# Reordering the first half of an attention kernel around its loads, splitting the third products, and moving three x copies to ScalarE

## The chip, the cores and the metric

The kernel runs on one core of one Trainium2 chip. The metric is the device time of one execution in microseconds (us). Every run also gives a span, from the first to the last instruction that the profile shows; it is 1.7 to 3.4 us shorter than the device time. Times inside a trace count from the start of the span. A run counts as slow when it lies more than 1.5% above the fastest of the same kernel in its call; comparisons use fast runs unless the text says otherwise.

## The reference, cut to what matters

A linear attention with a decay per head (4 batches, 8 heads, 768 positions, head width 64), whose output, as x of 4 x 768 x 512, goes through a token mixer. The kernel computes the attention in chunks of 128 positions.

```python
for b in range(nb):                      # blocks of positions
    intra = ((qb @ kb^T) * Dmask) @ vb
    inter = (qb * lam_pow) @ kv_state
    out[block] = intra + inter
    kv_state = lam_block * kv_state + (kb * rev_pow)^T @ vb
# ... x = out, heads side by side
wq, wk = x @ w_q, x @ w_k                # 512 -> 64
W_tok  = 1/sqrt(64) * wq @ wk^T          # 768 x 768, per batch
out    = relu(W_tok @ x) @ w_out
```

The kernel computes (wq wk^T) x as wq (wk^T x): **py** is wk^T x, its copy is **Y**, and the "third products" **pm** are Y times wq.

## The kernel before

One loop step n handles one pair of heads; there are 16 steps, four for each batch. `kk` is the place of the pair in its batch. The pieces, with the names by which the profile's rows show them:

- `load_more` issues on GpSimd the loads of q, k and v of a pair (fq, fk, fv) and scales v of an earlier pair (vn).
- `turn(n)` transposes q and k on TensorE (trq, trk); VectorE copies q (qT), ScalarE copies k (kT).
- `states(n)` (dps), `scores(n)` (sc, then four masks by VectorE into pr), `inter(n)` (first part of oa), `values(n)` (rest of oa, copied to xnat by ScalarE), `flip(n)` (xp, transposed x, copied to xT).
- The mixer: `mix_wk` (the k projection, wk), `mix_wq`, `mix_py`, `mix_pm` and the output products `mix_po` (po).

```python
def load_more(n):
    load_q(n)
    load_kv(n, "k")
    scale_v(n - 2, nc.gpsimd) if n - 2 > 3 else None
    load_kv(n, "v")

def flip(n):
    b, kk = pairs[n]
    xp = pst([128, NCH, CH], BF16, "xp")
    for t in range(NCH):
        nc.tensor.transpose(xp[:, t, :], xnat[b][:, t, kk * CH : (kk + 1) * CH], ident)
    # ... last pair: half on each engine
    elif n < 2:
        nc.scalar.copy(out=to, in_=xp)
    else:
        nc.vector.tensor_copy(out=to, in_=xp)

def mix_pm(b, which, ...):          # two values of "which" are four products, in four banks
    pms = [pst([128, HALF], F32, "pm") for _ in which]
    # ... one matmul each from Y and wqT, then a ScalarE relu of each into rmT

for n in range(N):
    b, kk = pairs[n]
    if 8 <= n + 6 < N:
        load_more(n + 6)
    # ...
    p = b - 1
    third = [2 * kk - 4, 2 * kk - 3] if b >= 1 and kk >= 2 else []
    outs = ...                      # which output products go into this step
    if n >= 1 and not third:
        inter(n - 1)
    scores(n)
    if n >= 1 and third:
        inter(n - 1)
    if third:
        mix_pm(p, third)
    masks(n, 0)
    masks(n, 1)
    if n >= 1:
        values(n - 1)
    if n >= 2:
        flip(n - 2)
    for i, t in outs:
        mix_po(i, t)
    if b >= 1 and kk == 1:
        mix_wk(p)
    if n <= 9:
        states(n)
        turn(n + 1)
    if 9 <= n < N - 1:
        states(n + 1)
    if 9 <= n < N - 2:
        turn(n + 2)
    # ...
    if b >= 1 and kk == 1:
        mix_wq(p)
        mix_py(p)
```

The order of the calls is the order of the instructions on every engine. Up to step 9 the turn of pair n+1 is the last thing of step n; step 9 is the "double step", which does the states and turns of two pairs, so that from step 10 on the turn runs two pairs ahead of the scores. All PSUM tiles come from one pool of 8 banks.

## Time and profile before

| | before |
|---|---|
| device time, median of 3 | 108.0 us (107.91 to 109.81) |
| the profiled run: device time, span | 106.78, 105.1 us |
| busy share of TensorE, VectorE, ScalarE, GpSimd | 81%, 64%, 60%, 64% |
| scores of pair 8 start | 46.56 us |
| states of pair 10 start | 56.96 us |
| inter of pair 15 (start of the unchanged tail) | 86.56 us |

A line of an engine's timeline reads: start, length, engine, source line, operation, output <- inputs, shape, and how many instructions are grouped. The bracket gives the idle time just before and what ended it. In the list of waits a row has the total, the number of times and the longest. The lines of this kernel are read in the prediction below. One group is added: the third products of step 10 in TensorE's timeline of the kernel before.

```profile
59.30 0.51 PE L284 MATMUL sc<-qT,kT 64*128 64x128 bf16 x12
...
60.60 0.50 PE L437 MATMUL pm<-wqT,Y 64*128 64x384 bf16 x3 [0.44 <-ACT Y L420]
```

Scores and inter stand between py and the third products, and cover most of the time that ScalarE needs for Y. 0.44 us is left uncovered.

### The profile page before, as it was taken

Reading aid. Unit: us, or ns where it says so; the run is one execution under the profiler, and the core shown is the slowest. Engines: PE = TensorE matmul, PEld = TensorE weight load, DVE = VectorE, ACT = ScalarE, POOL = GpSimd, SP = SyncE. Lnnn points to the kernel's source line nnn. Section 1 sums busy time; section 2 is a strip of 40 time slices with the busy share of each in tenths; the row PEclk is TensorE's granted clock in tenths of the full one; section 3 lists DMA queues with packets and bytes.
Section 4 is the critical chain, followed back from the end, with each engine's and each line's share of the span. In section 5 each row is a group of like instructions: output and inputs, shape, how many; then the busy total and the mean of one; then the engine's idle time right before and its main releaser. Section 6 shows DMA issues by size and latency. Waiting matters only on the chain.

```text
span 105.1 us, 3513 instructions
## 1 busy us (share of the span) xinstructions
PE 85.0 (81%) x1496; PEld 57.1 (54%) x1504; DVE 67.1 (64%) x168; ACT 63.4 (60%) x124; POOL 67.5 (64%) x69
## 2 busy tenths in 40 slices
PE   4957898776559868979749998999498999999960
PEld 1325786655448555465549675567385548443430
DVE  3247997895886677257486689397768485237240
ACT  4282458657331996756632999766349796658430
POOL 5999999699999999999999999735000000000000
PEclk9996559999999999999999999999999999999998
DMA  0999999999999999999999999998930142342584
GB/s 21 261 174 160 163 166 166 173 164 168 197 170 164 168 155 158 149 136 163 128 137 138 136 154 133 136 263 296 372 148 0 54 152 100 127 172 104 225 312 158
DMA packets 67440, 17.12 MB, mean 163 GB/s; under 512 B 62946, under 2 KB 64482, under 8 KB 67426
## 3 DMA queue, kind: packets, MB, share of 16 engines
q0 software_dynamic: 60400, 9.57, 123.3%
q1 hardware_dynamic: 6882, 7.21, 20.3%
q8 instruction: 11, 0.18, 0.8%
q10 hardware_dynamic: 144, 0.13, 0.4%
q14 instruction: 3, 0.02, 0.1%
HBM read 20.19 MB, written 6.29 MB: 252 GB/s over the span
## 4 chain that ended last, share of the span: by engine, by line
PE 43%; POOL 16%; ACT 14%; DVE 13%; DMA 8%; issue 3%; ACTq 0%; POOLq 0%; DVEq 0%
PE po L475 18%; DVE pr L297 8%; DMA fv<-in_v_dram 8%; ACT kT L241 5%; POOL fv L78 4%; POOL fk L78 4%; PE dps L254 4%; PE oa L325 3%; POOL fq L73 3%; ACT rmT L457 3%; PE wk L366 3%; PE xp L344 3%; POOL vn L192 3%; PE trk L237 3%; PE trq L218 3%
## 5 line engine op out<-in xcount | busy, mean ns | idle before, releaser
L297 DVE TENSOR_TENSOR pr<-sc,maskc 128x384 bf16<-128x384 f32 x64 | 31.2, 550 | 8.3 <-PE sc L284 8.3
L241 ACT COPY kT<-trk 128x768 bf16<-128x768 bf16 x16 | 12.8, 799 | 19.1 <-PE trk L237 18.8
L192 POOL TENSOR_TENSOR vn<-fv,DvI 128x768 bf16<-128x768 bf16 x14 | 21.0, 1500 | 3.8 <-DMA fv<-in_v_dram 3.4
L475 PE MATMUL po<-wo,rmT 128*128 128x512 bf16 (+1 forms) x92 | 22.3, 370 | 0.5
L78 POOL DMA_DIRECT2D fv<-in_v_dram x16 | 17.3, 1081 | 0.8 <-POOLq L612 0.8
L485 ACT COPY osb<-po 128x512 f32<-128x512 f32 (+1 forms) x22 | 12.6, 579 | 8.3 <-PE po L475 8.2
L337 ACT CAST xnat<-oa 128x384 bf16<-128x384 f32 x31 | 13.5, 493 | 4.8 <-PE oa L325 4.6
L78 POOL DMA_DIRECT2D fk<-in_k_dram x15 | 15.6, 1041 | 0.0
L475 PEld LDWEIGHTS <-rmT 128*128 128x128 bf16 x100 | 9.0, 98 | 9.5 <-issue 0.8
L457 ACT ACTIVATE rmT<-pm 128x384 bf16<-128x384 f32 x28 | 11.7, 493 | 1.7 <-PE pm L437 1.6
L73 POOL DMA_DIRECT2D fq<-in_q_dram x15 | 12.7, 847 | 0.0
L284 PE MATMUL sc<-qT,kT 64*128 64x128 bf16 x192 | 8.7, 228 | 4.8 <-ACT kT L241 3.8
L284 PEld LDWEIGHTS <-kT 64*128 64x128 bf16 x192 | 6.1, 99 | 6.5 <-ACT kT L241 4.7
L218 PE MATMUL trq<-ident,fq 128*64 128x128 bf16 x192 | 9.0, 231 | 0.6 <-DVE fq L501 0.6
L224 DVE TENSOR_TENSOR qT<-trq,dq 128x768 bf16<-128x768 bf16 x16 | 8.8, 549 | 0.9 <-PE trq L218 0.9
L325 PE MATMUL oa<-vn,pr 128*128 128x64 bf16 x192 | 8.7, 197 | 0.0
L325 PEld LDWEIGHTS <-pr 128*128 128x128 bf16 x192 | 6.7, 100 | 3.5 <-issue 2.6
L237 PE MATMUL trk<-ident,fk 128*64 128x128 bf16 x180 | 8.0, 226 | 0.7 <-DMA fk<-in_k_dram 0.7
L437 PE MATMUL pm<-wqT,Y 64*128 64x384 bf16 x32 | 6.8, 327 | 2.1 <-ACT Y L420 1.3
L264 DVE COPY two<-dps 128x64 f32<-128x64 f32 x16 | 3.5, 218 | 7.7 <-PE dps L254 7.7
L352 DVE COPY xT<-xp 128x768 bf16<-128x768 bf16 x13 | 7.2, 552 | 1.5 <-PE xp L344 1.5
L344 PE MATMUL xp<-ident,xnat 128*128 128x128 bf16 x96 | 8.0, 219 | 0.0
(61 smaller groups left out, 110.7 us busy)
## 6 DMA issues: line engine op xcount, KB each, us to landing
out_dram<-osb SPq DMA_DIRECT2D x23, 256.0 KB, 2.1
fv<-in_v_dram POOLq DMA_DIRECT2D x16, 192.0 KB, 6.2
fq<-in_q_dram POOLq DMA_DIRECT2D x15, 192.0 KB, 5.7
fk<-in_k_dram POOLq DMA_DIRECT2D x15, 192.0 KB, 6.1
wo<-in_moe_w_out_dram POOLq DMA_DIRECT2D x1, 512.0 KB, 7.9
k<-in_k_dram SPq DMA_DIRECT2D x1, 384.0 KB, 3.6
q<-in_q_dram SPq DMA_DIRECT2D x1, 384.0 KB, 5.4
wqk_f<-in_moe_w_q_dram SPq DMA_DIRECT2D x1, 128.0 KB, 6.4
```

The costliest lines, as they stand in the source:

```text
L73: nc.gpsimd.dma_start(out=t, in_=q_rows(n))
L78: nc.gpsimd.dma_start(out=t, in_=kv_rows(n, dict(k=k, v=v)[nm]))
L192: eng.tensor_tensor(out=vn, in0=staged.pop((n, "v")), in1=DvI[:, 2 * kk : 2 * kk + 2, :].unsqueeze(3).to_broadcast([128, 2, NCH, D]), op=A ...
L218: nc.tensor.transpose(trq[hl * 64 : hl * 64 + 64, 2 * a : 2 * a + 2, r, :], fq[:, hl, a, r * D : (r + 1) * D], ident,)
L241: nc.scalar.copy(out=kT, in_=trk)
L284: nc.tensor.matmul(sc[a, hl][:, cc, :], kT[r, c * CH : (c + 1) * CH], qchunk(n, r, c), start=True, stop=True, skip_group_check=True,)
L297: nc.vector.tensor_tensor(out=t, in0=L[n]["sc"][a, hl], in1=maskc, op=ALU.mult)
L325: nc.tensor.matmul(oa[hl][:, c, :], pr[c // 3, hl][:, c % 3, :], vn[:, hl, c, :], start=False, stop=(c == NCH - 1), skip_group_check=True,)
L337: nc.scalar.copy(out=to, in_=oa[hl])
L457: nc.scalar.activation(out=to, in_=pm, func=ACT.Relu, scale=1.0 / 8.0)
L475: nc.tensor.matmul(po, M[b]["rmT"][:, kt, t * CH : (t + 1) * CH], wo[:, kt, c : c + w], start=(kt == 0), stop=(kt == 3),)
L485: nc.scalar.copy(out=osb[:, c : c + w], in_=po)
```

## The change

The intent is to put work that needs nothing new between a transposition and the reader of its copy, so that TensorE does not wait for copies, and to feed the mixer's projections earlier. There are five parts. No instruction is added or taken away; three x copies change from VectorE to ScalarE (steps 4, 9 and 13).

1. In steps 1 to 3 and 5 to 7, states and turn come ahead of values, flip and po ("the whole-array phase behind the turn").
2. The first k projection moves from step 5 to step 4, its wq and py into the middle of step 5. For this, x of pair 3 is turned in step 4 already, and x of pair 2 is copied by ScalarE.
3. The double step moves from 9 to 8, one po from 8 to 9.
4. In steps 9 and 13 x is turned before values and copied by ScalarE. In step 13, too, a po now stands ahead of wk: it is taken from step 14.
5. In steps where kk is 2 or 3, half of the third products stand ahead of scores and half behind inter.

```diff
-    def flip(n):
+    def flip(n, eng=None):
...
-        elif n < 2:
+        elif eng is nc.scalar:
             nc.scalar.copy(out=to, in_=xp)
...
-        third = [2 * kk - 4, 2 * kk - 3] if b >= 1 and kk >= 2 else []
-        outs = {7: [...], 8: [(0, 3), (0, 4), (0, 5)], N - 1: [(2, 0)]}.get(n)
+        outs = {7: [...], 8: [(0, 3), (0, 4)], 9: [(0, 5)], 10: [], N - 1: [(2, 0)]}.get(n)
...
-            outs = [..., [], [(p - 1, 4), (p - 1, 5)], ...][kk]
+            outs = [..., [(p - 1, 4)], [(p - 1, 5)], ...][kk]
...
+        def back():
+            if kk == 1 and n > 8:
+                flip(n - 2, nc.scalar)
+            if n >= 1:
+                values(n - 1)
+            if n >= 2 and not (kk == 1 and n > 8) and n != 5:
+                flip(n - 2, nc.scalar if n < 5 else None)
+            if n == 4:
+                flip(n - 1)
+            for i, t in outs:
+                mix_po(i, t)
+            if kk == 1 and n > 8:
+                mix_wk(p)
-        if n >= 1 and not third:
+        if n >= 1 and not (b >= 1 and kk >= 2):
             inter(n - 1)
-        scores(n)
-        if n >= 1 and third:
+            scores(n)
+        elif n >= 1:
+            mix_pm(p, [2 * kk - 4])
+            scores(n)
             inter(n - 1)
-        if third:
-            mix_pm(p, third)
+            mix_pm(p, [2 * kk - 3])
+        else:
+            scores(n)
         masks(n, 0)
         masks(n, 1)
-        # values, flip, outs, mix_wk stood here
-        if n <= 9:
+        if n == 4 or n >= 8:
+            back()
+        if n <= 8:
             states(n)
+        if n == 5:
+            mix_wq(p)
+            mix_py(p)
+        if n <= 8:
             turn(n + 1)
-        if 9 <= n < N - 1:
+        if 8 <= n < N - 1:
             states(n + 1)
-        if 9 <= n < N - 2:
+        if 8 <= n < N - 2:
             turn(n + 2)
...
-        if b >= 1 and kk == 1:
+        if kk == 1 and n > 8:
             mix_wq(p)
             mix_py(p)
+        if n == 4:
+            mix_wk(p)
+        elif n < 8:
+            back()
```

More of the change, by code (lines that the diff above doesn't have):

```diff
@@ L531 @@
         p = b - 1
-        third = [2 * kk - 4, 2 * kk - 3] if b >= 1 and kk >= 2 else []
-        outs = {7: [(0, 0), (0, 1), (0, 2)], 8: [(0, 3), (0, 4), (0, 5)], N - 1: [(2, 0)]}.get(n)
-        if outs is None:
-            outs = [
-                [(p - 1, 2), (p - 1, 3)],
-                [],
-                [(p - 1, 4), (p - 1, 5)],
-                [(p, 0), (p, 1)],
-            ][kk]
-            outs = [(i, t) for i, t in outs if i > 0]
-        if n >= 1 and not third:
+        outs = {
+            7: [(0, 0), (0, 1), (0, 2)],
+            8: [(0, 3), (0, 4)],
+            9: [(0, 5)],
+            10: [],
+            N - 1: [(2, 0)],
+        }.get(n)
+        if outs is None:
+            outs = [[(p - 1, 2), (p - 1, 3)], [(p - 1, 4)], [(p - 1, 5)], [(p, 0), (p, 1)]][kk]
+            outs = [(i, t) for i, t in outs if i >= 0]
+        def back():
[12 more added lines that the diff above has]
+        if n >= 1 and not (b >= 1 and kk >= 2):
             inter(n - 1)
-        scores(n)
-        if n >= 1 and third:
+            scores(n)
+        elif n >= 1:
+            mix_pm(p, [2 * kk - 4])
+            scores(n)
             inter(n - 1)
-        if third:
-            mix_pm(p, third)
+            mix_pm(p, [2 * kk - 3])
+        else:
+            scores(n)
         masks(n, 0)
         masks(n, 1)
-        if n >= 1:
-            values(n - 1)
-        if n >= 2:
-            flip(n - 2)
-        for i, t in outs:
-            mix_po(i, t)
-        if b >= 1 and kk == 1:
-            mix_wk(p)
-        if n <= 9:
+        if n == 4 or n >= 8:
+            back()
+        if n <= 8:
             states(n)
+        if n == 5:
+            mix_wq(p)
+            mix_py(p)
+        if n <= 8:
             turn(n + 1)
-        if 9 <= n < N - 1:
+        if 8 <= n < N - 1:
             states(n + 1)
-        if 9 <= n < N - 2:
+        if 8 <= n < N - 2:
             turn(n + 2)
@@ L573 @@
             make_dq(3)
-        if b >= 1 and kk == 1:
+        if kk == 1 and n > 8:
             mix_wq(p)
             mix_py(p)
+        if n == 4:
+            mix_wk(p)
+        elif n < 8:
+            back()
     bl = B - 1
```

## The prediction

> **What bounds the kernel now.** I read the busy tenths first, then the chain that ended last, then the waits, then TensorE's timeline step by step. One loop step n handles one pair of heads; the 16 steps fill 9.1 to 86.6 us, the tail after them is not changed.
>
> From the page (busy tenths in 40 slices of 2.6 us; then the chain by engine):
>
> ```profile
> PE   4957898776559868979749998999498999999960
> ...
> POOL 5999999699999999999999999735000000000000
> ...
> PE 43%; POOL 16%; ACT 14%; DVE 13%; DMA 8%; issue 3%; ACTq 0%; POOLq 0%; DVEq 0%
> ```
>
> GpSimd is full to slice 25 (67 us) and then stops; TensorE has holes until slice 30 and is full after that. So there are two regimes: loads first, TensorE's queue later. The chain agrees: its DMA and GpSimd parts all end at 26.8 us. GpSimd issues the loads and scales v; its timeline gives the time from which the state products of a pair can start (start, duration; 2nd line is pair 4, 4th pair 9, last pair 15):
>
> ```profile
> 20.18 1.47 POOL L192 TENSOR_TENSOR vn<-fv,DvI 128x768 bf16<-128x768 bf16 x1 [1.00 <-DMA fv<-in_v_dram]
> ...
> 25.26 1.52 POOL L192 TENSOR_TENSOR vn<-fv,DvI 128x768 bf16<-128x768 bf16 x1
> ...
> 29.59 1.51 POOL L192 TENSOR_TENSOR vn<-fv,DvI 128x768 bf16<-128x768 bf16 x1
> ...
> 47.33 1.50 POOL L192 TENSOR_TENSOR vn<-fv,DvI 128x768 bf16<-128x768 bf16 x1
> ...
> 71.03 1.47 POOL L192 TENSOR_TENSOR vn<-fv,DvI 128x768 bf16<-128x768 bf16 x1 [1.83 <-DMA fv<-in_v_dram]
> ```
>
> One every 4.33 us. State products of pair 4 started at 26.83, at once; those of pairs 5, 6, 7, 8, 9, 10 at 32.46, 37.34, 44.49, 50.38, 56.01, 56.96, that is 1.4, 1.5, 4.3, 5.9, 7.2 and 3.8 us after their v. TensorE loses ground to the loads from step 5 on, and this lag is what a better order can win back. Where it is lost, TensorE's timeline of steps 8 and 9 (start, us; brackets: idle and what ended it):
>
> ```profile
> 51.00 0.50 PE L237 MATMUL trk<-ident,fk 128*64 128x128 bf16 x12
> 51.43 0.44 PE L307 MATMUL oa<-gs,qT 64*128 64x64 bf16 x10
> 52.45 0.51 PE L284 MATMUL sc<-qT,kT 64*128 64x128 bf16 x12 [0.58 <-ACT kT L241]
> 52.89 0.52 PE L325 MATMUL oa<-vn,pr 128*128 128x64 bf16 x12
> 53.25 0.50 PE L344 MATMUL xp<-ident,xnat 128*128 128x128 bf16 x6
> 53.59 0.25 PE L366 MATMUL wk<-wqk,xT 128*128 128x64 bf16 x3
> 55.30 0.79 PE L366 MATMUL wk<-wqk,xT 128*128 128x64 bf16 x21 [1.46 <-DVE xT L352]
> ```
>
> and the waits from 28 to 86 us (total, times, longest):
>
> ```profile
> PE wk L366 <- DVE xT L352: 4.4, 3, 1.5
> ...
> PE sc L284 <- ACT kT L241: 2.6, 4, 1.0
> ...
> PE pm L437 <- ACT Y L420: 1.3, 3, 0.4
> ```
>
> Three costs show. Scores follow their own k turn directly and wait for ScalarE's copy (0.80 us). The k projection wk needs x turned (xT), whose VectorE copy is queued behind four masks of 0.47 us each. And wk, wq, py and the Y copies stand in one row. A fourth is inside a group, in step 11:
>
> ```profile
> 63.21 0.31 PE L307 MATMUL oa<-gs,qT 64*128 64x64 bf16 x10
> 63.66 1.25 PE L437 MATMUL pm<-wqT,Y 64*128 64x384 bf16 x4
> 64.84 0.52 PE L325 MATMUL oa<-vn,pr 128*128 128x64 bf16 x12
> ```
>
> Four third products (pm) take 0.64 us where they flow (93.85 on); here 1.6 us pass from 63.21 to 64.84, where 0.16 for oa and 0.64 would do: 0.8 us lost.
>
> **What the Trainium skill says.** "TensorE: Matmul & The Clock Gate", section "Architectural detail": matmuls stay in program order, ScalarE and VectorE are strict FIFO. The trace agrees: nothing passes wk during its 1.46 us, though the loaded states and turns stand behind it. "PSUM — Partial Sum Buffer", Specifications: 8 banks per partition. The kernel has one pool of 8; 4 scores + 2 oa + 4 pm is 10, and the trace names a mask (a reader of sc) as what ended a pm's wait at 40.4. "VectorE: DVE Perf Modes", the TRN2 errata section: PSUM source to SBUF (120 + N/2)/0.96 on VectorE for 16 bits, (172 + N)/1.2 on ScalarE; N = 768 gives 525 and 783 ns, measured 548 and 817. So moving an x copy to ScalarE costs 0.3 us more of engine time.
>
> **The change, part by part.** No instruction is added or removed; the work of TensorE stays.
>
> *1. Steps 1-7 but 4: states and turn before values, flip and output products.* About 0.7 us of values and flip (step 7: and 2.6 us of po) now cover the kT copy. But states(n) now needs its v earlier in the step. Steps 1-3 gain nothing: the k of pair 4 lands at 23.2 (the turn waited 0.74 us for it), and scores(4) stays at 24.7. In step 4 two x copies and the wqk cast sit in ScalarE's queue: kT to 24.65, xnat(2) to 25.4, xT(1) to 26.2, wqk to 26.75, xnat(3) to 27.5. So flip(3) starts at 27.55, turn(5) ends 28.9, scores(5) at 29.8: 0.9 later than now.
>
> *2. wk of batch 0 in step 4, wq and py in step 5.* wk at 28.9, wkn by 30.2. states(5) wait for v to 31.1, then wq to 32.05, py to 32.8, Y by 34.0, k turn copied 34.8: scores(6) at 34.85, no gain on 34.81. The 1.46 us hole of step 5 only became a load wait and a ScalarE row. From here it pays: states(6) 36.5, scores(7) 38.55 (now 39.41), states(7) 40.2 = v of pair 7, po after the turn, scores(8) 44.65 (now 46.56): **1.9 us** ahead.
>
> *3. Double step at 8 in place of 9, one po moved from 8 to 9.* states(9) wait for v, 48.85; scores(9) at 50.0 (now 52.45).
>
> *4. x copied by ScalarE ahead of values in steps 9 and 13.* flip at 50.3, ScalarE free at 50.9, copy done 51.7; values and a po (0.86) fill in; wk at 51.9 without a wait. That takes 1.46 us off in each of steps 9 and 13. In step 9 about 0.7 goes to v of pair 10, ready 53.16: states(10) 53.2 (now 56.96).
>
> *5. pm on both sides of scores.* 2 + 4 + 2 banks fit in 8. Steps 11 and 15: most of 0.8 us each is won. Steps 10 and 14 lose: pm now stands right behind py and waits for all three Y copies, 60.56 - 59.3 = 1.25 us instead of 0.44: minus 0.8 each.
>
> Walking on with the same durations (states 0.28, turn 0.68, inter 0.16, scores 0.35, values 0.36, flip 0.34, po 0.86, wk 0.72, wq 0.65, py 0.75) I get scores(10) 57.1 (now 59.30), scores(12) 65.4 (68.57), scores(13) 69.25 (72.72), states(14) 71.9 (76.28), states(15) 78.45 (82.88), inter(15) 82.0 (86.56). **Sum: 4.5 us**, against 105.1 span. As a ledger from step 5: +1.9 by step 8, +0.6 to scores(9), +1.3 to states(10) after the load wait, -0.8, +0.75, +1.46, -0.8, and the rest through po's under waits.
>
> **Rivals.** *The loads keep it.* If states sit hard on GpSimd's 4.33 us rhythm, all gain before 53 us is capped at the lags above (3.8 us at pair 10), and only part 4 of step 13 and part 5 remain: still 3 us or more. v of pairs 11 to 15 is 4 to 10 us early, so loads cannot bind later. For a bigger loss, loads would have to be slowed; GpSimd's order is not touched. *ScalarE or VectorE becomes the bound.* In steps 5-15 VectorE has about 40 us of work (3.55 a step), ScalarE about 38, in 57.7 us that would shrink to 53: 75%. Not a bound on average, but step 10's masks start late behind pm's Y wait, and VectorE then has masks, xT, gs, qT, masks in a row: 1 to 2 us of the gain could go; time 105 to 106. *Too little bank room*: oa now lives until values behind the turn; inter(6) waits for it (I counted 0.1 to 0.4 us). With several such waits, 1 us. *All hidden*: no gain would need the tail bound by something else; but from 86.6 us TensorE is full (9s), so an earlier start moves the end.
>
> **Range and chances.** 108.0 - 4.5 = 103.5; such walks miss small new waits, so I take 0.4 back: 103.9. Low 102.0: the Y wait is covered and each step gains more. High 106.3: ScalarE's queue in step 4 and the masks of step 10 eat 2.5 us. The 2% line is 105.84, gain 2.2 us: faster 0.84, same 0.13, slower 0.03.
>
> **What would show it.** Right: states of pairs 5, 7, 9, 10 start within 0.1 us of their v; wk in steps 9 and 13 idles under 0.2 us; scores(8) near 44.7; the four pm of steps 11 and 15 flow; pm behind py idles about 1.2 us twice; inter(15) near 82, tail still 18.5 us. Wrong: GpSimd's scalings later than now, scores(5) later than 30.2, flip(3) waiting past 28, or a loss in step 10 that is not won back in 11.

## The result

| | before | after |
|---|---|---|
| device time, median of 4 | 108.91 us (107.91 to 110.87) | 103.25 us (103.04 to 104.18) |
| ratio of the fast runs, 95% interval | | 0.9581 (0.9482 to 0.968) |
| span of the profiled run | 105.1 us | 101.3 us |

A ratio here is the mean time of one kernel's fast runs over the mean of the other's fast runs of the same rounds, so it is not quite the ratio of the medians: two of the four runs of before counted as slow.

From the page of the kernel after (busy tenths in 40 slices of 2.5 us, then the chain by engine):

```profile
PE   4986989768698687999999699999988899999950
...
POOL 5999999899999399999999999992140000000000
...
PE 35%; POOL 27%; DMA 17%; ACT 12%; issue 4%; DVE 1%; POOLq 0%; ACTq 0%
```

TensorE shows 8 or 9 tenths from slice 17 (41 us) to slice 38, with one hole of 6 in slice 23 (56 to 58 us, the waits of step 10); before, it had holes until slice 29. The chain that ended last has moved: GpSimd and the DMA transfers, 24% of it before, are now 44%, and VectorE has all but left it. The timeline of GpSimd in the kernel after shows the scalings of pairs 6, 7 and 10:

```profile
34.76 1.47 POOL L192 TENSOR_TENSOR vn<-fv,DvI 128x768 bf16<-128x768 bf16 x1 [1.52 <-PE pm L437]
...
39.09 1.51 POOL L192 TENSOR_TENSOR vn<-fv,DvI 128x768 bf16<-128x768 bf16 x1
...
52.06 1.51 POOL L192 TENSOR_TENSOR vn<-fv,DvI 128x768 bf16<-128x768 bf16 x1
```

They end at 40.6 for pair 7 and 53.57 for pair 10. The wait of 1.52 us ahead of pair 6 is put down to a pm, the last event before it, but this scaling needs nothing from pm: in four of the other traces the same wait is put down to the landing of v (fv), which is the likely cause here too. TensorE's timeline of the kernel after has the states groups of pairs 7 and 10 each 0.06 us behind these ends, and step 9 between them:

```profile
40.66 0.42 PE L254 MATMUL dps<-vn,fk 128*64 128x128 bf16 x9 [0.57 <-POOL vn L192]
...
50.51 0.50 PE L284 MATMUL sc<-qT,kT 64*128 64x128 bf16 x12
50.99 0.49 PE L344 MATMUL xp<-ident,xnat 128*128 128x128 bf16 x6
51.32 0.51 PE L325 MATMUL oa<-vn,pr 128*128 128x64 bf16 x12
51.67 1.03 PE L475 MATMUL po<-wo,rmT 128*128 128x512 bf16 x3
52.54 0.86 PE L366 MATMUL wk<-wqk,xT 128*128 128x64 bf16 x24
53.63 0.42 PE L254 MATMUL dps<-vn,fk 128*64 128x128 bf16 x9 [0.23 <-POOL vn L192]
```

All 24 wk run in one group with no bracket; before, three ran and 21 waited 1.46 us. The scores wait for nothing. The next lines are the same timeline, first step 10 behind py, then step 11:

```profile
55.20 0.85 PE L405 MATMUL py<-xnat,wkn 128*64 128x256 bf16 x12
56.52 0.33 PE L437 MATMUL pm<-wqT,Y 64*128 64x384 bf16 x1 [0.46 <-ACT Y L414]
57.28 0.33 PE L437 MATMUL pm<-wqT,Y 64*128 64x384 bf16 x1 [0.43 <-ACT Y L420]
...
60.29 0.34 PE L437 MATMUL pm<-wqT,Y 64*128 64x384 bf16 x2
60.46 0.72 PE L284 MATMUL sc<-qT,kT 64*128 64x128 bf16 x12
61.30 0.32 PE L307 MATMUL oa<-gs,qT 64*128 64x64 bf16 x10
61.70 0.39 PE L437 MATMUL pm<-wqT,Y 64*128 64x384 bf16 x2
```

In step 10 the first two pm now wait for Y twice, and the scores stand behind them. In step 11 the pairs of pm flow, but the scores group between them takes 0.72 us instead of 0.50, and 0.40 us pass from inter at 61.30 to the second pair. The waits of the kernel after, same stretch as in the prediction (28 to 86 us), confirm the exchange:

```profile
PE dps L254 <- POOL vn L192: 1.0, 3, 0.6
PE trk L237 <- DMA fk<-in_k_dram: 0.9, 1, 0.9
PE pm L437 <- ACT Y L414: 0.9, 2, 0.5
PE pm L437 <- ACT Y L420: 0.9, 2, 0.4
...
PE sc L284 <- ACT kT L241: 0.2, 1, 0.2
```

The waits of scores for kT fell from 2.6 to 0.2 us and those of wk for xT from 4.4 to nothing. What came in their place are waits for loads (1.9 us) and for Y (1.8 instead of 1.3).

Stage by stage, in us (start of each group; "predicted" is the walk of the prediction; the last column is what the change won within the stage):

| group | before | predicted | after | won in the stage |
|---|---|---|---|---|
| scores(8) | 46.56 | 44.65 | 45.24 | 1.32 |
| states(10) | 56.96 | 53.2 | 53.63 | 2.01 |
| states(11), end of step 10 | 61.82 | | 59.24 | -0.75 |
| scores(12) | 68.57 | 65.4 | 65.74 | 0.25 |
| scores(13) | 72.72 | 69.25 | 69.89 | 0.00 |
| states(14) | 76.28 | 71.9 | 72.72 | 0.73 |
| states(15) | 82.88 | 78.45 | 79.19 | 0.13 |
| inter(15) | 86.56 | 82.0 | 82.77 | 0.10 |
| end of the span | 105.1 | 100.6 | 101.3 | 0.0 |

In step 13 the hole of 1.46 us goes, but the po taken from step 14 comes in, so the row of states(14) shows half of it; the row of states(15) has the rest, and the loss by pm in step 14.

The traces differ by 3.8 us, the fast runs by 4.5 (107.95 mean before, times 1 - 0.9581). The profiled run of before, at 106.78 us, was itself 1.2 us faster than the fast runs against which the ratio is taken.

### The profile page after: what moved, and what is told of

Same layout as the page of the kernel before. It is cut to its first block, busy times and chain, and to the rows that moved or that the text cites.

```text
span 101.3 us, 3514 instructions
## 1 busy us (share of the span) xinstructions
PE 86.3 (85%) x1494; PEld 58.5 (58%) x1504; DVE 65.4 (65%) x165; ACT 65.3 (65%) x127; POOL 67.5 (67%) x69
## 4 chain that ended last, share of the span: by engine, by line
PE 35%; POOL 27%; DMA 17%; ACT 12%; issue 4%; DVE 1%; POOLq 0%; ACTq 0%
PE po L475 14%; DMA fk<-in_k_dram 10%; POOL vn L192 7%; DMA fv<-in_v_dram 7%; POOL fk L78 6%; POOL fv L78 6%; POOL fq L73 5%; ACT rmT L457 5%; PE oa L325 3%; ACT kT L241 3%; PE xp L344 3%; PE dps L254 3%; PE trk L237 3%; PE pm L437 2%; PE trq L218 2%
## 5 line engine op out<-in xcount | busy, mean ns | idle before, releaser
L457 ACT ACTIVATE rmT<-pm 128x384 bf16<-128x384 f32 x28 | 12.2, 499 | 0.4 <-PE pm L437 0.2
L284 PE MATMUL sc<-qT,kT 64*128 64x128 bf16 x192 | 9.8, 228 | 1.8 <-DVE qT L224 0.9
L218 PE MATMUL trq<-ident,fq 128*64 128x128 bf16 x192 | 9.6, 237 | 0.2
L284 PEld LDWEIGHTS <-kT 64*128 64x128 bf16 x192 | 6.8, 99 | 3.3 <-issue 1.5
L254 PE MATMUL dps<-vn,fk 128*64 128x128 bf16 (+2 forms) x150 | 6.9, 224 | 1.7 <-POOL vn L192 1.0
L254 PEld LDWEIGHTS <-fk 128*64 128x64 bf16 x150 | 5.4, 113 | 4.8 <-issue 1.4
```

What stands on the lines that cost most here:

```text
L254: nc.tensor.matmul(dps[hl * 64 : hl * 64 + 64, c:end, :], kn[:, hl, c, :], vn[:, hl, c, :].unsqueeze(1).to_broadcast([128, end - c, D]), s ...
L284: nc.tensor.matmul(sc[a, hl][:, cc, :], kT[r, c * CH : (c + 1) * CH], qchunk(n, r, c), start=True, stop=True, skip_group_check=True,)
L457: nc.scalar.activation(out=to, in_=pm, func=ACT.Relu, scale=1.0 / 8.0)
```

## The experiments

Twelve kernels ran, in three calls on three chips. An edit is shown against the changed kernel unless it says otherwise. The times in the expectations are for the span of the profiled run. The kernel before was noisy (106.72 to 109.51, 107.05 to 111.5, 107.4 to 112.93 us; of its seven runs four, three and five counted as slow). So the verdict on each of the twelve ratios stayed "unclear", and I rest on the spans and stages of the profiled runs, with the ratios beside them. The theory at the outset was the prediction's walk: each of the five parts is worth what it says there. The rival was that the loads hold the first half whatever the order does.

One caution for all comparisons of two profiled runs: the loads do not land at the same time in every run. Seven of the kernels (the changed one, x_on_vector, pm_late_10_14, pm_late_7_11_15, double_at_9, late_v_after and proj_before_turn) are the same up to the scaling of v of pair 6, yet it starts anywhere between 34.26 and 34.78 us, and the v of every pair up to 10 shifts with it. A difference of up to 0.5 us between two traces can be this alone. The mean span of all fast runs of a kernel evens it out in part: 101.2 us for the changed kernel.

### x_on_vector: undo part 4

VectorE copies x in steps 9 and 13, and x is turned after values; the po still stands ahead of wk.

```diff
-            if kk == 1 and n > 8:
-                flip(n - 2, nc.scalar)
...
-            if n >= 2 and not (kk == 1 and n > 8) and n != 5:
+            if n >= 2 and n != 5:
```

> The changed kernel with its fourth part undone: in steps 9 and 13 x is copied by VectorE after the masks and the values stand first again. Theory: the k projection waits for the copy behind four masks again. Step 9: masks end at 52.8, copy at 53.3, wk 0.8 us later than now, of which the wait for v of pair 10 (53.6) hides some 0.3; step 13: 0.8 us later. Span 101.3 + 1.3 = 102.6. Rival: the one output product that now stands between (0.86 us) covers the wait by itself and the engine does not matter: 101.3 within 0.2.

Measured: median 104.39 us (104.17 to 104.75), ratio 0.9705 (0.9611 to 0.9799), span 102.3. TensorE's timeline of this kernel, step 9:

```profile
53.22 0.79 PE L366 MATMUL wk<-wqk,xT 128*128 128x64 bf16 x21 [0.60 <-DVE xT L352]
```

The wait is back, at 0.60 us in each of the two steps. The old hole of 1.46 us is thus covered by two things: 0.86 by the po that the change moves ahead of wk, 0.60 by the ScalarE copy together with turning x ahead of values (no run separates these two). In step 9 part of the loss is taken up by the wait for v of pair 10 (states(10) at 53.94, 0.31 later). The wait is 0.60 us where 0.8 was expected; otherwise the theory held.

### pm_late_10_14: undo part 5 in steps 10 and 14

```diff
+        elif n >= 1 and n in (10, 14):
+            scores(n)
+            inter(n - 1)
+            mix_pm(p, [2 * kk - 4, 2 * kk - 3])
         elif n >= 1:
             mix_pm(p, [2 * kk - 4])
```

> The changed kernel, but in steps 10 and 14 all four third products again behind scores and inter, so that these 0.5 us of work lie inside the wait for the Y copies. Theory: part five costs there what I said, so this is faster: values(9) at about 57.9 instead of 58.45, the same in step 14, span 101.3 - 1.1 = 100.2. Rival: 4 + 2 + 4 banks do not fit in 8, the last two pm wait for masks and the gain is eaten: 101.3 within 0.3.

Measured: median 101.75 us (101.0 to 101.9), ratio 0.9442 (0.934 to 0.9544), span 99.4. TensorE's timeline of this kernel, step 10:

```profile
55.69 0.51 PE L284 MATMUL sc<-qT,kT 64*128 64x128 bf16 x12
...
56.99 0.49 PE L437 MATMUL pm<-wqT,Y 64*128 64x384 bf16 x3 [0.43 <-ACT Y L420]
```

Scores start behind py at once, and one wait of 0.43 us is left, as before the change. Step 10, from states(10) to states(11), takes 4.88 us (5.61 in the changed kernel, 4.86 before); states(14) to states(15) takes 5.74 (6.47). So each of the two costs 0.73 us. Together that is 1.46 of the 1.9 us between the spans; of the rest, 0.3 stood at states(10) already, where v of pair 10 came earlier. The gain of 1.9 is more than the 1.1 expected. This is the fastest version that ran: it beats both kernels.

### pm_late_7_11_15: undo part 5 in steps 7, 11 and 15

```diff
+        elif n >= 1 and kk == 3:
+            scores(n)
+            inter(n - 1)
+            mix_pm(p, [2 * kk - 4, 2 * kk - 3])
```

> The changed kernel, but in steps 7, 11 and 15 all four third products behind scores and inter, as before. Theory: bank waits come back, 0.6 to 0.8 us in each of steps 11 and 15; step 7 is hidden by the wait for v of pair 7. Span 101.3 + 1.4 = 102.7. Rival: the split only moves the wait from pm to inter (the trace shows inter waiting 0.2 us for a bank in step 15), so no more than 0.4: 101.3 to 101.7.

Measured: median 103.48 us (103.36 to 103.93), ratio 0.9613 (0.9501 to 0.9725), span 101.6. TensorE's timeline of this kernel, step 11:

```profile
60.01 0.51 PE L284 MATMUL sc<-qT,kT 64*128 64x128 bf16 x12
60.36 0.52 PE L307 MATMUL oa<-gs,qT 64*128 64x64 bf16 x10
61.02 1.25 PE L437 MATMUL pm<-wqT,Y 64*128 64x384 bf16 x4
```

The stretched pm group of 1.25 us is back, yet step 11 (states(11) to states(12)) grows only from 5.29 to 5.76, and step 15 (states(15) to inter(15)) from 3.58 to 3.68. The split is worth 0.47 and 0.10 us, 0.57 in all; the spans differ by only 0.3 because v of pair 10, and with it states(10), came 0.28 earlier in this run. The rival was right: most of what pm no longer waits for, scores and inter wait for. In step 15 this is shown: inter waited 0.21 us for ScalarE's relu of pm, whose bank it takes. For step 11 it is argued: the lines above show scores at 0.72 us, and the trace names only one cause, 0.17 us in which a weight load of scores waited for VectorE's gs, the last reader of the bank of dps.

### back_first_567: undo part 1 in steps 5 to 7

```diff
-        if n == 4 or n >= 8:
+        if n >= 4:
             back()
...
-        elif n < 8:
+        elif n < 4:
             back()
```

> The changed kernel, but in steps 5, 6 and 7 the whole-array phase (values, flip, output products) ahead of states and turn, as before; the k projection stays in step 4. Theory: the first half is bound by v (states of pair 7 started 0.1 us after its v), the output products of step 7 merely change places with a wait, and scores(8) comes at 45.2 as now: span 101.3 within 0.3. Rival: this order is what won the first half, by covering the k copies: scores(8) 1.0 to 1.9 us later, span 102.3 to 103.2.

Measured: median 103.72 us (103.25 to 104.19), ratio 0.9639 (0.9537 to 0.9742), span 101.7. Scores(8) start at 45.99 (0.75 later), but states(10) at 54.04 without a wait (0.41 later), and the span is 0.4 longer. About half of the loss is absorbed where the changed kernel waits for v of pair 10. But v of pair 10 was ready at 53.14 in this run, 0.43 earlier than in the changed kernel, so measured from its v the states start 0.90 us late instead of 0.06. The mean span is 101.8, 0.6 longer. The result lies between the theory and the rival.

### double_at_9: undo the double step of part 3 (the po stays in step 9)

```diff
-        if n <= 8:                  # both places
+        if n <= 9:
...
-        if 8 <= n < N - 1:          # likewise for turn
+        if 9 <= n < N - 1:
```

> The changed kernel with its third part undone: the step that does two pairs of states and turns is 9 again, not 8. Theory: v of pair 10 (ready at 53.6) hides nearly all of it; scores(9) then waits 0.8 us for its k copy, wk comes at 52.3 as now, but states(9) and turn(10), 1.0 us, stand between it and states(10), which starts at 54.0 instead of 53.6. Span 101.3 + 0.4 = 101.7. Rival: the wait for the k copy and the crowded step 9 show in full, as in the kernel before: 1.0 us or more, span 102.3 up.

Measured: median 103.45 us (103.09 to 103.59), ratio 0.9631 (0.9565 to 0.9696), span 101.1. Scores(9) wait 0.58 us for kT again, and states(10) start at 53.51, no later than in the changed kernel. Yet a loss of 0.4 is there, hidden by earlier loads. GpSimd's scaling of pair 10 and the states of pair 10 in this kernel:

```profile
51.60 1.50 POOL L192 TENSOR_TENSOR vn<-fv,DvI 128x768 bf16<-128x768 bf16 x1
...
53.51 0.42 PE L254 MATMUL dps<-vn,fk 128*64 128x128 bf16 x10
```

v was ready at 53.10, 0.47 earlier than in the changed kernel (53.57), though the edit touches nothing ahead of step 8. States(10) come 0.41 us behind it and have no bracket: here the order holds them and not v, as the theory has it for 0.4. Over all runs the mean span is 101.4 against 101.2. So this trace shows 0.4 us and the mean of the runs 0.1; which is nearer is not settled.

### k_proj_step5: undo part 2

This edit does a little more than undo part 2: with it step 4 has states and turn first, and step 5 has values and flip first.

```diff
-            if n == 4:
-                flip(n - 1)
...
-            if kk == 1 and n > 8:
+            if kk == 1 and n > 4:
                 mix_wk(p)
...
-        if n == 4 or n >= 8:
+        if n == 5 or n >= 8:
             back()
...
-        if n == 5:                  # and mix_wq, mix_py move to the end of step 5
-            mix_wq(p)
-            mix_py(p)
...
-        if n == 4:
-            mix_wk(p)
-        elif n < 8:
+        if n < 8 and n != 5:
             back()
```

> The changed kernel with its second part undone: first k projection in step 5 (values and flip first there, x of pair 3 by VectorE), wq and py at the end of step 5. Theory: the hole behind the masks of step 5 returns (1.4 us), Y is ready only at 36.1, and the first pm, which now stands ahead of scores(6), holds it to 36.4 (now 34.98); part of that is won back in the wait for v of pair 7 (40.5), scores(8) about 1.0 us later. Span 101.3 + 0.9 = 102.2. Rival: the loads (pair 7 and 10) take all of it: 101.3 to 101.6.

Measured: median 103.26 us (103.02 to 103.42), ratio 0.9616 (0.9554 to 0.9679), span 101.2. Scores(6) start 1.1 us later (36.08), scores(8) 0.34 later (45.58), states(10) at 53.61, as in the changed kernel. Here too v of pair 10 came early (53.18), and states(10) are 0.43 us behind it. The mean span is 101.3. My expectation of 0.9 was wrong; the rival, that the loads absorb it, fits the span, but not all of it is absorbed by v of pair 10 in this trace.

The last three runs together say that parts 1, 2 and 3 largely stand in for each other: taking out one of them alone costs 0.6, 0.1 and 0.1 us in the mean spans, and 0.84, 0.37 and 0.35 us more lag behind v of pair 10 in the traces, because what they win ahead of about 53.5 us ends at that v.

### first_half_only: the change up to step 7, the old order from step 8

The edit puts the old lists of po, the old x copy, the double step at 9, and all pm behind inter for n above 8:

```diff
-            if kk == 1 and n > 8:
-                flip(n - 2, nc.scalar)
...
+        elif n >= 1 and n > 8:
+            scores(n)
+            inter(n - 1)
+            mix_pm(p, [2 * kk - 4, 2 * kk - 3])
...
-        if n <= 8:
+        if n <= 9:
```

> The change up to step 7 alone, from step 8 on all as before (third part, x copies, order of pm and output products). Theory: scores(8) comes at 45.2 instead of 46.56 and the 1.3 us stay to the end, because the loads are 4 us and more early from there: span 105.1 - 1.3 = 103.8. The other 2.5 us come from step 8 on. Rival: the first half made room that only the second half uses; alone it is worth under 0.5: 104.6 or more.

Measured: median 105.31 us (105.1 to 105.44), ratio 0.9803 (0.9725 to 0.9881), span 103.0. Scores(8) start at 44.55, 2.0 us ahead of before, and from there to inter(15) 39.99 us pass, against 40.0 before. That is more than the 1.3 expected. So a gain of the first half does stay to the end when it isn't run into the next load; it was 2.0 us here (1.3 in the profiled run of the changed kernel, where v of pair 6 was scaled 0.7 us later).

### second_half_only: the old order to step 7, the change from step 8

This edit is against the kernel before; it takes over parts 3 to 5 for n of 8 and more.

```diff
+            if kk == 1 and n > 8:
+                flip(n - 2, nc.scalar)
...
+        elif n >= 1 and n < 8:
+            scores(n)
             inter(n - 1)
+            mix_pm(p, [2 * kk - 4, 2 * kk - 3])
```

> The kernel before up to step 7, the change from step 8 on (double step at 8, x by ScalarE with an output product ahead of wk in 9 and 13, pm on both sides in 10, 11, 14, 15). Theory: the halves stand in for each other ahead of the floor at pair 10. scores(8) at 46.6 as before, states(10) at 54.7 instead of 56.96, and the 0.5 us of steps 10 to 15 on top: span 105.1 - 2.8 = 102.3, though the first half alone already gave 2.1 of 3.8. Rival: the halves add up, so this gives 3.8 - 2.1 = 1.7: 103.4.

Measured: median 106.08 us (104.11 to 108.23), ratio 0.9723 (0.9419 to 1.0027). The interval holds everything from 6% faster to no difference, and the profiled run counted as slow (span 104.6, clock 0.917). Its two fast runs have spans of 102.1 and 103.4, one at the theory's figure and one at the rival's. I draw no conclusion from it.

### no_scale_after: no scaling of v by GpSimd from pair 4 on

This kernel gives a wrong result (relative error 0.858). It takes the scaling out to see whether it is GpSimd's work that holds states(7) and states(10).

```diff
-        scale_v(n - 2, nc.gpsimd) if n - 2 > 3 else None
+        if n - 2 > 3:
+            L[n - 2]["vn"] = staged.pop((n - 2, "v"))
...
-            scale_v(n + 4, nc.gpsimd)
+            L[n + 4]["vn"] = staged.pop((n + 4, "v"))
```

> Wrong result on purpose: the changed kernel without GpSimd's scaling of v from pair 4 on, the loaded v is used as it is. GpSimd then issues loads every 2.9 us instead of 4.33. Theory: the changed kernel touches the loads at pairs 7 and 10 only (TensorE waited 0.6, 0.2 and less there), so with v early the span falls by 0.8 to 1.2: 100.1 to 100.5, unless faster issue only queues in the DMA engines. Rival: the loads hold the whole first half, every state product follows its v: steps 6 to 10 shrink by more than 2 us, span below 99.3.

Measured: median 103.85 us (103.79 to 104.08), ratio 0.9677 (0.9616 to 0.9738), span 101.9, so not faster than the changed kernel. The waits for v are gone and states(7) and states(10) start 0.97 and 0.55 us earlier (39.69 and 53.08). But from 30 to 56 us the transfers move 164 GB/s where they moved 151, with GpSimd busy 77% of that stretch instead of 94%, and a v load takes 9.2 us from issue to landing instead of 5.8: with GpSimd out of the way, the transfers set the rhythm. A v load is issued every 3.7 us (31.91 to 46.62 us), not every 2.9 as expected. And TensorE's timeline of this kernel shows stops within one group of transpositions:

```profile
40.77 0.47 PE L219 MATMUL trq<-ident,fq 128*64 128x128 bf16 x10 [0.58 <-issue]
...
54.81 0.25 PE L219 MATMUL trq<-ident,fq 128*64 128x128 bf16 x2 [1.00 <-issue]
```

"issue" means that the profile shows nothing that TensorE waited for. Counting its matmuls and weight loads, such stops (one more of 0.68 us, before 34.02) come after 957, 1213 and 1725 instructions, that is 256 and 512 apart. The first is not new: pm_late_7_11_15, double_at_9, first_half_only and late_v_after stop after the same 957 instructions, for 0.45, 0.78, 0.54 and 0.99 us; the other two stand in this kernel alone. This fits a fetch of instructions in blocks of 256 that sometimes comes late; that is argued from the counts, and no run tested it. The theory held for the waits and failed for the time.

### late_v_after and late_v_before: make v of pair 7 late in either kernel

One more multiplication of the same size (1.5 us) on GpSimd behind the scaling of pair 6, so that all later loads and scalings come that much later. The edit is the same in both kernels:

```diff
         scale_v(n - 2, nc.gpsimd) if n - 2 > 3 else None
+        if n == 8:
+            extra = consts.tile([128, 2, NCH, D], BF16, name="extra")
+            nc.gpsimd.tensor_tensor(out=extra, in0=L[n - 2]["vn"], in1=DvI[...], op=ALU.mult)
```

> The changed kernel with one more GpSimd multiply (1.5 us, into a tile nobody reads) behind the scaling of v of pair 6, so that the v of every later pair comes 1.4 us later. Theory: in the changed kernel TensorE meets v at pairs 7 and 10 (waits of 0.6 and 0.2 us) and this is the floor under all that is done ahead of step 10; states(10) moves from 53.6 to 55.0, and the span by 1.2 to 1.4: 102.5 to 102.7. Rival: TensorE's own work is the bound and the waits for v are chance: 101.3 to 101.8.

> The kernel before with the same extra 1.5 us on GpSimd. Theory: its states run 3.8 us and more behind v from pair 7 on, so nothing is felt: ratio to the kernel before 1.00 within 0.005, span 105.1 within 0.3. Rival: v is a bound there too: 1.01 or more.

Measured on the changed kernel: median 106.13 us (105.67 to 106.4), ratio 0.9856 (0.9763 to 0.9949), span 103.7, which is 2.4 longer; more than expected. From its TensorE timeline (source lines are 8 higher here), and below that from its windows, the stretch 44.0 to 46.5 us with busy times of the engines, the clock (0.50), the DMA share and GB/s:

```profile
41.78 0.42 PE L262 MATMUL dps<-vn,fk 128*64 128x128 bf16 x9 [1.86 <-POOL vn L192]
```

```profile
44.00:46.50 2.50, 2.50 (x8) 0.87 (x6) 0.56 (x1) 1.14 (x3) 2.50 (x3) 0.50 1.87 143
```

States(7) wait 1.86 us instead of 0.57 and start 1.1 later. Soon after, the clock of TensorE is halved, and the group of 12 po takes 4.16 us instead of 2.75: 1.4 us more. The two make up the 2.46 us by which inter(15) is late. So the late v itself cost 1.1 us, near the 1.2 to 1.4 expected; that it also brought the slower clock is not shown, though all four runs of this kernel have spans of 103.7 to 104.5.

Measured on the kernel before: median 108.23 us (107.13 to 110.3), ratio 1.0009 (0.9845 to 1.0173). Its states(7) start at 47.24 with no bracket, 5 us behind v. The interval is wide, and would not exclude a loss of 1.4 us, and the profiled run counted as slow. What carries the point is the fast trace of the kernel before: its states(7) start 4.3 us behind their v, more than the 1.5 us added. So it has slack against the loads at this place, the changed one has none.

### proj_before_turn: pm_late_10_14, with wq and py ahead of the turn in steps 9 and 13

```diff
+        if kk == 1 and n > 8:       # now between states(n + 1) and turn(n + 2)
+            mix_wq(p)
+            mix_py(p)
```

> A version meant to beat both: the changed kernel with all four pm behind scores and inter in steps 10 and 14, and in steps 9 and 13 wq and py ahead of the turn, as the change itself has it in step 5, so that turn, scores and inter (1.2 us) cover the Y copies and the k copy no longer delays them. Theory: the 0.43 us wait for Y in steps 10 and 14 goes; the banks (4 scores, 2 oa, the turn's 2) then make pm wait for masks, so only 0.2 to 0.6 each is won over the version with late pm (span 99.4): 98.3 to 99.0. Rival: the banks eat all: 99.4 within 0.2.

Measured: median 102.33 us (101.94 to 102.91), ratio 0.9499 (0.9394 to 0.9605), span 100.0. It is not better than pm_late_10_14 (99.4, on another chip), and the expectation of 98.3 to 99.0 missed. Step 10 takes 5.00 us against 4.88, states(14) to states(15) 5.86 against 5.74. The turn covers the Y copies, but now three pm wait 0.37 us for the kT copy, which holds the bank that they need. The wait for data became a wait for room.

## Why the prediction was right or wrong

The time came out at 103.25 us, 0.65 below the figure predicted and inside the range, and faster was the likeliest class. By its own steps:

- **Parts 1 and 2, scores from step 5 on: right in place, half a microsecond off.** Scores(5), (6) and (7) started at 29.73, 34.98 and 38.59 (predicted 29.8, 34.85, 38.55). For scores(6) this was partly luck: the walk had py end at 32.8 and ScalarE's row of copies hold kT until 34.8; py ended at about 32.0, but the k of pair 6 landed late, TensorE waited 0.95 us for it (to 33.50), and ScalarE stood idle for 0.73 us before it copied kT, to 34.93. The miss is states(7), 40.66 instead of 40.2: v of pair 6 was scaled only at 34.76, after a wait of 1.52 us, 0.43 later than in the trace of before, and pair 7 followed on its 4.33 us. This shift lies within the spread of the loads over the runs (34.07 to 34.78), so it does not count for or against the change. Scores(8) at 45.24 inherit that.
- **Part 2, "From here it pays", with 1.9 us at scores(8): the gain is real, its attribution was not.** 1.3 us came in the profiled run, but taking out part 2 alone costs 0.1 us in the mean span (k_proj_step5), the double step alone 0.1 (double_at_9), part 1 in steps 5 to 7 alone 0.6 (back_first_567). A walk that adds each part in turn does not say what each is worth, since v of pair 10 caps their sum.
- **Part 3: right.** Scores(9) at 50.51, states(9) at 49.30 (predicted 50.0, 48.85), both carrying the 0.4 us by which v came later.
- **Part 4: right.** wk has no wait in step 9 or 13; x_on_vector shows the split of the 1.46 us, 0.86 by the po, as in the walk, and 0.60 by the earlier ScalarE copy.
- **Part 5, steps 10 and 14, "minus 0.8 each": right.** 0.73 us each (pm_late_10_14), in two waits for Y of 0.46 and 0.43 us.
- **Part 5, steps 11 and 15, "most of 0.8 us each is won": wrong in size.** 0.47 and 0.10 us (pm_late_7_11_15). The step counted the stretched pm group as pure loss (its own reading was even on the low side: six pm of the tail take 0.79 us, so four that flow take 0.53, not 0.64). But the banks that pm waits for are needed by scores and inter as well, so splitting pm moves a part of the wait onto them (named by the trace in step 15, argued for step 11). This was the rival "too little bank room", which I had sized for inter(6) alone.
- **The sum, 4.5 us: 0.7 too much for the trace,** 3.8 between the two spans (inter(15) at 82.77 against 82.0). 0.4 of the 0.77 stood at states(10), which now wait for v at 53.57 instead of 53.16: the loads again. The remaining 0.3 did not come where the split of pm paid less: from states(10) to scores(12) the walk has 12.2 us and the trace 12.11, because the walk's own times lose 0.6 us there, where its ledger (-0.8 and +0.75) loses almost nothing. It came in step 12, scores(12) to scores(13), for which the walk has 3.85 us and both kernels 4.15. Nothing was changed in that step; the sum of single durations missed small gaps between groups (values, for instance, follow the start of scores after 0.43 us, not 0.35). That the median still fell below the prediction is not to the walk's credit: the walk came from a trace of 106.78 us and was taken off a median of 108.0.
- **The signs.** Two of those named for "wrong" came true: GpSimd's scalings were later than before for pairs 6 to 13 (by 0.4 us, within the spread of the loads), and the 0.75 us lost in step 10 were not won back in step 11 (0.25). Of those for "right", the four states groups at their v, wk without a wait and the tail of 18.5 us came true; the pm of steps 11 and 15 did not flow, and pm behind py idled 0.9 us in all instead of 1.2.
- **The rivals.** "The loads keep it" was right up to states(10) and wrong after, as the prediction had it: the changed kernel waits for v at pairs 5, 7 and 10. VectorE and ScalarE did not become the bound (65% each).

That late_v_after loses time, while the kernel before has 4.3 us of slack behind the same v, is the sign for the regime: the order has won back most of the lag behind the loads, and what was won ahead of pair 10 met the same floor near 53.5 us. The prediction's 525 and 783 ns for an x copy are estimates from the formula of the page that it names; the 548 and 817 ns of the traces are used. Its "program order" for matmuls stands in Part 2 of the page named, not in "Architectural detail". What stays open is whether the noise of the kernel before (6 us between its fastest and slowest run over all calls, against 1.1 us for the changed kernel in its one call) also has to do with that lag; no run of comparable state tests it.

## What to carry to other kernels

First find the floor, here the time at which each pair's v is ready; several reorderings ahead of a floor are not worth the sum of their parts, and each can be tested by taking it out alone. Place work that needs nothing new between a producer and the reader of its copied result, and never put the reader right behind the producer as step 10 does: undoing that alone gave the best version, 101.75 us, 0.944 of the time before. When a wait for a buffer is removed by moving its group, look who takes that buffer next, since the wait may move there.

## What the Trainium skill lacked or had wrong

- "TensorE: Matmul & The Clock Gate", Part 1: the page has the clock drop after at least one idle window, about 3.4 us. In late_v_after a single wait of 1.86 us, which ended at 41.78 us, was followed by a granted clock of 0.50 from 44.0 to 46.5 us and 12 po at 4.16 us instead of 2.75, and one of 1.34 us, which ended at 23.00, by a clock of 0.50 from 23 to 26 us. The eight waits of 1.45 or 1.46 us in before, first_half_only and late_v_before were followed by nothing of the kind. So a drop can come after about half of the idle time given or less, and the length of one wait does not decide it; no run tests what does. (The page's section on a second failure mode has frequent short idles do it too, but gives no length.)
- The same page, Part 1, says that the trace's clock records have been seen to be unreliable. That is right: the record gives the changed kernel's profiled run a mean clock of 1.0, although its 12 k transpositions take 0.85 us at 11.75 us and 0.50 us at 19.01.
- "Advanced Engine Details and Errata", ISA Cache: the page gives a cache line of 256 instructions, but no cost for getting the next one; "Runtime: NRT & Kernel Launch", "Instruction fetch mechanics", calls the cost of crossing such a block mostly hidden. TensorE stopped with no cause in the profile after 957 instructions in five kernels (0.45 to 0.99 us), and after 1213 and 1725 in no_scale_after (0.58 and 1.00 us). If these are such fetches, which no run tests, their cost was not hidden there.
- No page that I read has it that the bank of a finished matmul can pass a wait from one group to another when groups are reordered: the split of pm was worth 0.57 us where the prediction had read 0.8 us of loss in each of the two stretched groups.
